# A fused attention and two-MLP kernel: the second half of w1 decoded earlier and kept in DRAM, the second half of w2 decoded beside the last two units

## The chip, the core and the metric

The kernel runs on one core of one Trainium2 chip. TensorE (PE) multiplies, VectorE (DVE), ScalarE (ACT) and GpSimd (POOL) work on tiles, and SyncE (SP) issues nearly all DMAs, in order, from one queue. The metric is the time of one execution on the device in microseconds (us).

## The reference, cut to what matters

```python
attn_out = attention(q, k, v, M_prev, z_prev, beta)      # 4 x 8 heads x 576 x 64
x = attn_out.transpose(0, 2, 1, 3).reshape(2304, 512)
h = x @ w_in                                             # 512 x 2048
g = h * tanh(softplus(h))
x = g @ w_out                                            # 2048 x 512
a, b = x @ w1, x @ w2                                    # 512 x 1024 each
out = ((a * b) @ w3) @ w_out2                            # 1024 x 1024, 1024 x 512
```

Inputs and weights of the two MLPs come as float64 words, and the kernel works on float32. "Decoding" a piece of a weight means turning its 128x512 words of 64 bits into float32.

## The kernel before, in words

All matrix products are made from split numbers: a weight or an activation is kept as a high part and a low part, and each product is three matmuls (high by high, low by high, high by low).

*Decoding.* `decode` loads one piece (`draw`, 512 KB) from SP's queue, runs six DVE instructions on it (lines 113, 115, 117, 120, 124, 126) and one add on POOL (line 131). What follows depends on the use. `to_split` makes the high part (line 76) and the low part (line 79) on POOL, straight into a weight tile. `to_dram` makes both on POOL, into the raw buffer itself, and writes them to a DRAM scratch tensor (line 161), from where `from_dram` loads them later (line 657) with no further work.

*First stage.* Attention over 16 pairs of heads; it leaves x, split, in two tiles with the tags `xs0` and `xs1`.

*Second stage.* Units (g, n): g is one of four quarters of w_in and w_out, n one of six chunks of 384 tokens. `emit_h` makes h for a unit (48 matmuls), ACT and DVE turn it into y, `emit_x2` multiplies by w_out for the unit before it (48 matmuls) and DVE adds the result into `x2` (line 604). Beside the units of a quarter the next quarter's eight pieces are decoded (`nextq`), and at fixed units one or two pieces of `predecode` (`pre`): w_out2, the first half of w1 and the first half of w2, 16 pieces in all, into DRAM. So a unit has two or three decodes.

*Last quarter (g = 3).* There are no more quarters to decode. Instead `fold` multiplies w3 by w_out2 in 17 steps: a step decodes a piece of w3 (`da`), transposes it on PE (line 628), splits it (`w3h`, `w3l`), and multiplies the piece of the step before by `o2` (w_out2, loaded from DRAM, line 614). The finished rows go through `wo` to `w_dram`, and are loaded again as `wft` (line 702). `steps(beside, 1)` in `emit_h` and `emit_x2` advances the fold. When the unit n = 3 comes, the slot `xs0` is free, and the first halves of w1 and w2 are loaded into it (`w_slot(0)`).

*Last stage.* For each of 40 pairs (chunk c of 512 tokens, m one of 8 blocks of 128 columns), `emit_ab` makes a and b (24 matmuls into one of two `psA` tiles), ACT and DVE multiply and split them into one of six slots of `ring`, and `emit_out`, five pairs later, multiplies by `wft`. The pairs m = 4 to 7 need the second halves of w1 and w2 (tile `w12t`, slot `xs1`). In the kernel before these eight pieces are decoded by `rest`, two at the last `emit_x2` and two after each of the pairs k = 0, 1 and 2, first the four of w2, then the four of w1:

```python
        if k < 3:
            steps(rest, 1)
```

The split of the next token chunk (`x2s`, line 731) lies in memory that the decode buffers hold until `rest` is done.

*Order.* The framework moves instructions: each engine's order is set by a model of the run in which ready work of an earlier place in the program goes first, unless `tc.issue_after` holds it back. A change in one stage can therefore move instructions in the others. On the chip each engine then works through its list in order and waits on semaphores.

Of the kernel before, what the change touches and what calls it, by code (L numbers as in the profile page):

```python
# [9 lines left out]
F32 = mybir.dt.float32  # L10
# [11 lines left out]
def fused_kernel(ctx: ExitStack, tc, q, k, v, M_prev, z_prev, beta, w_in, w_out, w1, w2, w3, w_out2, out):  # L22
    nc = tc.nc
    B, H, S, D = q.shape
    NT, DM = out.shape
# [4 lines left out]
    KD = DM // 128  # L30
# [5 lines left out]
    NCH = NT // CH  # L36
# [4 lines left out]
    dram = ctx.enter_context(tc.tile_pool(name="dram", bufs=1, space=bass.MemoryType.DRAM))  # L41
# [14 lines left out]
    def f(ap):  # L56
        return ap.bitcast(F32)
# [26 lines left out]
    def steps(gen, n):  # L84

        for _ in range(n):
            next(gen, None)
# [5 lines left out]
    WN = 512  # L93
# [40 lines left out]
    def run(jobs, n):  # L134

        jobs = list(islice(jobs, n))
        for (a, r), (_, done) in zip(decode([src for src, _ in jobs]), jobs):
            done(a, r)

    def by_two(jobs):  # L140
        for _ in range(4):
            run(jobs, 2)
            yield

    def words(w, r0, c0):
        return w[r0:r0 + 128, c0:c0 + dec["w"]].bitcast(I32)

    def to_split(hi, lo):
        def done(a, r):
            pool_round(hi, a)  # L150
            sub(lo, a, hi, nc.gpsimd)

        return done

    def to_dram(dst):
        def done(a, r):
            w = dec["w"]
            hi, lo = r[:, 0:w], r[:, w:2 * w]
            pool_round(hi.bitcast(F32R), a)
            nc.gpsimd.tensor_tensor(out=lo.bitcast(F32R), in0=a, in1=hi, op=ALU.subtract)  # L160
            dm(out=dst.rearrange("i p c -> p i c"), in_=r.rearrange("p (i c) -> p i c", i=2))

        return done
# [11 lines left out]
    w1_dram = dram.tile([2, DM, WN], F32, name="w1_dram")  # L175
    o2_dram = dram.tile([2, FF2, DM], F32, name="o2_dram")
    w2_dram = dram.tile([2, DM, WN], F32, name="w2_dram")

    def predecode():
        for w, wd in ((w_out2, o2_dram), (w1, w1_dram), (w2, w2_dram)):  # L180
            for c in range(w.shape[0] // 128):
                yield words(w, 128 * c, 0), to_dram(wd[:, 128 * c:128 * c + 128, 0:WN])

    def second_half(t):
        for i, w in ((1, w2), (0, w1)):
            for c in range(KD):
                yield words(w, 128 * c, WN), to_split(t[:, i, 0, c], t[:, i, 1, c])

    xl = {}

# [464 lines left out]
    def from_dram(t, d):  # L655
        for i in range(2):
            dm(out=f(t[:, i]), in_=d[i].rearrange("(k p) f -> p k f", p=128))

    def w_slot(s):
        t = xp.tile([128, 2, 2, KD, 512], F32R, tag=f"xs{s}", name="w12t", padded_shape=[128, 2, 2, KD, S])  # L660
        if s == 0:
            for i, wd in enumerate((w1_dram, w2_dram)):
                from_dram(t[:, i], wd)
        w1t[s], w2t[s] = t[:, 0], t[:, 1]
        return t

    folding = fold()
    pre0 = nextq = iter(())
    prev = None
    w1t, w2t = [None, None], [None, None]  # L670
    for u in [(g, n) for g in range(NQ) for n in range(NCH)]:
        g, n = u
        last = g == NQ - 1
        if u not in gt:
            if last and fpool[0] is None:
                dk.close()
                fpool[0] = fk.enter_context(tc.tile_pool(name="fp", bufs=1))
                decoder(fk, 2, 2)
            y = early.pop(u) if u in early else emit_h(u, folding if last and n > 0 else iter(()))
        if last and n == 3:  # L680
            w_slot(0)
        if prev is not None:
            with tc.issue_after(emit_x2(prev, folding if last and n > 0 else pre0)):
                split = split_y(u, y)
        with tc.issue_after(split):
            if n == 0 and not last:
                run(pre, 2)
            elif not last:
                run(nextq if n < 4 else chain(islice(nextq, 1), islice(pre, 1)), 2)
            if g in (1, 2) and n in (0, 2):  # L690
                run(pre, 1)
        if last and n == 0:
            steps(folding, 1)
        if not last and n == 0:
            nextq = load_quarter(g + 1)
        prev = u
# [4 lines left out]
    for s in range(4):  # L701
# [1 line left out]
            out=f(wft[:, 1, 2 * s:2 * s + 2]),  # L703
            in_=w_dram[256 * s:256 * s + 256, :].rearrange("(k p) f -> p k f", p=128),
        )
    rest = by_two(second_half(w_slot(1)))
    emit_x2(prev, islice(rest, 1))
    wk.close()


# [61 lines left out]
    for k, (c, m) in enumerate(work):  # L772
        if k == 4:
            fk.close()
            late = ctx.enter_context(tc.tile_pool(name="late", bufs=1))
            x2s = late.tile([128, 2, KD, 512], F32R, name="x2s")
            xs_[1] = x2s[:, 0], x2s[:, 1]
        emit_ab(k)
        if k in (3, 4):
            for i in range(4 * k - 12, 4 * k - 8):  # L780
                nc.scalar.copy(out=wft[:, 0, i], in_=f(wft[:, 1, i]))
                sub(wft[:, 1, i], f(wft[:, 1, i]), wft[:, 0, i])
        if k < 3:
            steps(rest, 1)
        if m == 5 and c + 1 < len(spans):
            split_x2(c + 1)
        if k >= LAG:
            emit_out(k - LAG)
# [34 lines left out]
```

## Time and profile before

| what | value |
|---|---|
| runs of the kernel | 1024.27, 1026.0 and 1026.07 us, median 1026.0 us |
| the profiled execution | 1024.95 us, its span 1023.2 us |
| PE busy | 977.8 us (96%) |
| DVE busy | 612.0 us (60%) |
| ACT busy | 500.7 us (49%) |
| POOL busy | 339.0 us (33%) |
| granted TensorE clock, mean | 0.988 |

The span is what the profiler sees from the first to the last instruction; the execution's own time is 1.75 us longer. Busy shares are means over stages with different limits, so the sections below go by stretches of the span. Times in the rows are microseconds from the span's start unless marked ns.

### The profile page before, as it was taken

The page shows a single profiled execution, that of the slowest core. Times are in us where ns is not written, and L with a number is a line of the kernel's source. Part 1 is how long each engine was busy: PE and PEld are TensorE (multiplying, and loading weights), DVE is VectorE, ACT ScalarE, POOL GpSimd, SP SyncE. Part 2 cuts the span into 40 slices and gives each one's busy share as a digit, 9 for nine tenths or more (in the row PEclk, how much of TensorE's full clock was granted, in tenths as well). Part 3 has the DMA queues.
Part 4 walks back from the last instruction along what each step waited for, and adds up shares of the span by engine and source line. Part 5 has one row for each costly group of instructions (what it writes and reads, how often), then busy time and mean ns, then how long its engine had stood idle before and what let it go on. Part 6 is the DMA issues. An engine that isn't in the chain of part 4 may idle for free.

```text
span 1023.2 us, 15086 instructions
## 1 busy us (share of the span) xinstructions
PE 977.8 (96%) x5584; PEld 829.1 (81%) x5584; DVE 612.0 (60%) x1364; ACT 500.7 (49%) x1016; POOL 339.0 (33%) x345
## 2 busy tenths in 40 slices
PE   5888999999899999999999999999979999999998
PEld 2555555566799999999999999988758888888897
DVE  4887667667685759885987567667973121121111
ACT  5577888885655555556565544442313221221212
POOL 6675555433555254544454112112540000000000
PEclk9899999999999999999999999999999999999999
DMA  7343333311232124223331662222410000100101
GB/s 157 96 110 71 71 87 74 77 27 42 103 124 80 65 83 145 98 89 106 121 103 63 247 232 80 75 78 101 156 41 1 21 21 1 42 1 1 42 1 62
DMA packets 93626, 81.73 MB, mean 80 GB/s; under 512 B 68720, under 2 KB 72816, under 8 KB 93552
## 3 DMA queue, kind: packets, MB, share of 16 engines
q1 hardware_dynamic: 92224, 80.44, 25.3%
q8 instruction: 44, 0.72, 0.3%
q10 hardware_dynamic: 1328, 0.33, 0.2%
q14 instruction: 30, 0.25, 0.1%
HBM read 65.54 MB, written 15.20 MB: 79 GB/s over the span
## 4 chain that ended last, share of the span: by engine, by line
PE 71%; DVE 12%; ACT 11%; DMA 2%; POOL 2%; issue 2%; SPq 0%; POOLq 0%; ACTq 0%; DVEq 0%
PE psA L63 37%; PE psX L63 16%; PE psF L63 14%; ACT s L378 5%; ACT pt L430 3%; DVE s L368 2%; PE psF L66 2%; DMA draw<-in_moe_w_dram 1%; DVE da L120 1%; PE psX L66 1%; DVE xt L79 1%; POOL da L131 1%; DVE draw L126 1%; DVE da L117 1%; DVE s L373 1%
## 5 line engine op out<-in xcount | busy, mean ns | idle before, releaser
L63 PE MATMUL psA<-xt,wqt 128*128 128x384 f32 x1152 | 207.5, 335 | 0.2
L131 POOL TENSOR_TENSOR da<-da,draw 128x512 f32<-128x512 f32 x72 | 102.2, 1426 | 312.8 <-DVE draw L126 261.9
L63 PEld LDWEIGHTS psA<-xt,wqt 128*128 128x128 f32 x1152 | 200.0, 188 | 2.4 <-DVE y L487 0.8
L63 PE MATMUL psX<-gh,wqt 128*128 128x384 f32 x480 | 122.4, 335 | 1.1 <-DVE x L604 1.1
L749 DVE TENSOR_TENSOR bs<-bs,psA 128x512 f32<-128x512 f32 (+1 forms) x40 | 25.3, 633 | 160.0 <-ACT bs L748 160.0
L63 PE MATMUL psA<-x2h,w12t 128*128 128x512 f32 (+1 forms) x384 | 107.1, 356 | 6.9 <-DVE bs L749 4.6
L748 ACT COPY bs<-psA 128x512 f32<-128x512 f32 (+1 forms) x40 | 21.8, 545 | 162.1 <-PE psA L63 152.2
L378 ACT ACTIVATE s<-s,acc 128x512 f32<-128x512 f32 (+2 forms) x144 | 85.5, 603 | 12.8 <-DVE acc L373 12.7
L63 PE MATMUL psA<-x2s,w12t 128*128 128x512 f32 x384 | 89.6, 389 | 0.0
L63 PEld LDWEIGHTS psX<-gh,wqt 128*128 128x128 f32 x480 | 86.9, 188 | 2.3 <-DVE x L604 1.4
L477 ACT ACTIVATE y<-psA 128x384 f32<-128x384 f32 x96 | 42.0, 490 | 91.1 <-PE psA L63 91.0
L63 PEld LDWEIGHTS psA<-x2h,w12t 128*128 128x128 f32 x384 | 68.3, 189 | 20.7 <-DVE bs L749 5.0
L63 PEld LDWEIGHTS psA<-x2s,w12t 128*128 128x128 f32 x384 | 72.1, 188 | 14.9
L373 DVE CUSTOM_DVE_ANT_0 s<-psA,mask 128x512 f32<-128x512 f32 (+2 forms) x144 | 63.4, 483 | 34.4 <-PE psA L63 34.3
L63 PE MATMUL psX<-gl,wqt 128*128 128x384 f32 x240 | 80.3, 335 | 0.0
L66 PEld LDWEIGHTS psF<-ident,s 128*128 128x128 f32 x400 | 46.3, 147 | 40.8 <-ACT pt L430 24.8
L63 PE MATMUL psF<-gh,wqt 128*128 128x384 f32 x288 | 73.1, 334 | 0.0
L66 PE MATMUL psF<-ident,s 128*128 128x128 f32 x400 | 63.2, 292 | 9.9 <-ACT pt L430 7.5
L487 DVE TENSOR_TENSOR y<-y,psA 128x384 f32<-128x384 f32 x96 | 48.7, 549 | 34.9 <-ACT y L485 34.9
L63 PE MATMUL psA<-room,w12t 128*128 128x512 f32 (+1 forms) x192 | 68.0, 354 | 0.0
L368 POOL TENSOR_SCALAR s<-s,sum,ogp 128x128 f32<-128x128 f32 (+1 forms) x64 | 53.1, 840 | 37.2 <-DVE sum L364 37.2
L430 ACT COPY pt<-psF 128x512 f32<-128x512 f32 (+1 forms) x112 | 56.8, 546 | 16.0 <-PE psF L66 16.0
(114 smaller groups left out, 1878.3 us busy)
## 6 DMA issues: line engine op xcount, KB each, us to landing
draw<-in_moe_w_dram SPq DMA_DIRECT2D x32, 512.0 KB, 3.8
draw<-in_moe_w_out_dram SPq DMA_DIRECT2D x24, 512.0 KB, 3.5
draw<-in_moe_w_in_dram SPq DMA_DIRECT2D x16, 512.0 KB, 4.0
out_dram<-ob SPq DMA_DIRECT2D x18, 256.0 KB, 2.0
raw<-in_q_dram SPq DMA_DIRECT2D x32, 128.0 KB, 2.8
raw<-in_v_dram SPq DMA_DIRECT2D x32, 128.0 KB, 2.6
o_dram<-draw SPq DMA_DIRECT2D x8, 512.0 KB, 2.8
w_dram<-draw SPq DMA_DIRECT2D x8, 512.0 KB, 2.8
```

Of the source, the lines that this page charges most:

```text
L63: tail[0] = nc.tensor.matmul(o, lhsT=l, rhs=r, start=start, stop=stop).ins
L66: tail[0] = nc.tensor.transpose(o, src, ident).ins
L79: return (eng or nc.vector).tensor_tensor(out=dst, in0=src, in1=f(hi), op=ALU.subtract)
L131: nc.gpsimd.tensor_tensor(out=a, in0=a, in1=lw.bitcast(F32), op=ALU.add)
L368: (nc.gpsimd if x in ON_POOL else nc.vector).tensor_scalar(out=s, in0=s, scalar1=d["sum"][:, x:x + 1], scalar2=og[:, x:x + 1], op0=ALU.mul ...
L373: nc.vector.tensor_tensor_reduce(out=s, in0=o, in1=m, op0=ALU.add, op1=ALU.min, scale=-scale, scalar=init, accum_out=a,)
L378: nc.scalar.activation(out=s, in_=s, func=AF.Exp, scale=-1.0, bias=a, accum_out=r)
L430: nc.scalar.copy(out=t[:, 0:n], in_=o[:, 0:n])
L477: nc.scalar.activation(out=y[m // 2][:, m % 2], in_=hp[m], func=AF.Tanh, scale=0.5)
L487: nc.vector.tensor_tensor(out=y[i][:, j], in0=y[i][:, j], in1=hp[2 * i + j], op=ALU.mult)
L748: nc.scalar.copy(out=bs, in_=pb)
L749: nc.vector.tensor_tensor(out=bs, in0=bs, in1=pa, op=ALU.mult)
```

## The change

The second half of w1 joins `predecode`: four more pieces are decoded in the second stage and written to a new DRAM tensor `w1b_dram`, and for them the units with a third decode are moved and become eight instead of four. `w_slot(1)` is now called at the last unit, n = 5, and loads w1's second half from DRAM. Only the four pieces of w2's second half are still decoded into their tile: two beside the second half of the `emit_x2` of the unit (3, 4), between two fold steps (the new generator `both`), and two in the `emit_x2` of (3, 5). The last stage no longer decodes.

```diff
     def by_two(jobs):
-        for _ in range(4):
+        for _ in range(2):
             run(jobs, 2)
             yield
...
+    w1b_dram = dram.tile([2, DM, WN], F32, name="w1b_dram")
...
     def predecode():
         for w, wd in ((w_out2, o2_dram), (w1, w1_dram), (w2, w2_dram)):
             for c in range(w.shape[0] // 128):
                 yield words(w, 128 * c, 0), to_dram(wd[:, 128 * c:128 * c + 128, 0:WN])
+        for c in range(KD):
+            yield words(w1, 128 * c, WN), to_dram(w1b_dram[:, 128 * c:128 * c + 128, 0:WN])
 
     def second_half(t):
-        for i, w in ((1, w2), (0, w1)):
-            for c in range(KD):
-                yield words(w, 128 * c, WN), to_split(t[:, i, 0, c], t[:, i, 1, c])
+        for c in range(KD):
+            yield words(w2, 128 * c, WN), to_split(t[:, 1, 0, c], t[:, 1, 1, c])
...
             for i, wd in enumerate((w1_dram, w2_dram)):
                 from_dram(t[:, i], wd)
+        else:
+            from_dram(t[:, 0], w1b_dram)
...
+    def both(a, b):
+        while True:
+            next(a, None)
+            yield
+            next(b, None)
+            next(a, None)
+            yield
...
         if last and n == 3:
             w_slot(0)
+        if last and n == NCH - 1:
+            rest = by_two(second_half(w_slot(1)))
+            beside = both(folding, rest)
         if prev is not None:
-            with tc.issue_after(emit_x2(prev, folding if last and n > 0 else pre0)):
+            with tc.issue_after(emit_x2(prev, beside if last and n > 0 else pre0)):
                 split = split_y(u, y)
...
-            if g in (1, 2) and n in (0, 2):
+            if g in (1, 2) and n == 0 or not last and n in (2, 4):
                 run(pre, 1)
...
-    rest = by_two(second_half(w_slot(1)))
-    emit_x2(prev, islice(rest, 1))
+    emit_x2(prev, rest)
     wk.close()
...
-        if k < 3:
-            steps(rest, 1)
```

The orders show three places. The first is PE's list in the last stage, where the first products with `wft` (`emit_out`) stand. Before, it is after the fourth pair of `emit_ab`, and the next pair's matmuls wait for POOL, which makes `w12t`:

```order
L63 MATMUL psA<-x2h,w12t 128x512
L63 MATMUL psX<-wft,room 128x512 [waits Activation_49]
L63 MATMUL psX<-wft,room 128x512 [waits DMAHW4_49,DVE_49]
L63 MATMUL psX<-wft,room 128x512
L63 MATMUL psF<-wft,room 128x512 [waits PE_49]
L63 MATMUL psF<-wft,room 128x512
L63 MATMUL psA<-x2h,w12t 128x512 [waits DVE_49,Pool_49]
L63 MATMUL psA<-room,w12t 128x512
L63 MATMUL psA<-x2h,w12t 128x512 [waits Pool_49] x2
```

In the changed kernel the same rows stand after the sixth pair (144 matmuls of `emit_ab` ahead of them instead of 96):

```order
L63 MATMUL psA<-x2h,w12t 128x512
L63 MATMUL psX<-wft,room 128x512 [waits Activation_49]
L63 MATMUL psX<-wft,room 128x512 [waits DMAHW5_49,DVE_49]
L63 MATMUL psX<-wft,room 128x512
L63 MATMUL psF<-wft,room 128x512 [waits PE_49]
L63 MATMUL psF<-wft,room 128x512 x2
L63 MATMUL psX<-wft,room 128x512 x3
L63 MATMUL psF<-wft,room 128x512 [waits PE_49,Activation_49]
L63 MATMUL psF<-wft,room 128x512 x2
L63 MATMUL psA<-x2h,w12t 128x512 [waits DVE_49]
```

Between the first `emit_ab` matmul and these rows PE now has three groups of 12 fold matmuls and two sets of four transposes; before it had two groups and one set, so the fold ends one step later.

The second place is DVE's list near the third pair of the last stage. Before, two decodes run there, with the split of `wft` between them, and three more follow:

```order
L113 TENSOR_SCALAR da<-draw 128x512
L126 SCALAR_TENSOR_TENSOR draw<-draw 128x512
L115 TENSOR_SCALAR da<-da 128x512
L117 TENSOR_SCALAR da<-da 128x512
L120 SCALAR_TENSOR_TENSOR da<-draw,da 128x512
L79 TENSOR_TENSOR wft<-wft 128x512 x2
L124 TENSOR_SCALAR draw<-da 128x512
L749 TENSOR_TENSOR bs<-bs,psA 128x512
```

Now these are the last two decodes, both of w2, and `wft` comes behind them:

```order
L113 TENSOR_SCALAR da<-draw 128x512
L764 TENSOR_TENSOR bs<-bs,psA 128x512
L126 SCALAR_TENSOR_TENSOR draw<-draw 128x512
L115 TENSOR_SCALAR da<-da 128x512
L79 TENSOR_TENSOR room<-bs,room 128x512
L117 TENSOR_SCALAR da<-da 128x512
L79 TENSOR_TENSOR w3l<-psF,w3h 128x512
L120 SCALAR_TENSOR_TENSOR da<-draw,da 128x512
L124 TENSOR_SCALAR draw<-da 128x512
L126 SCALAR_TENSOR_TENSOR draw<-draw 128x512
L764 TENSOR_TENSOR bs<-bs,psA 128x512
```

The third place is SP's list at the start of the last quarter. Before, the first piece of w3 (`draw`) is loaded ahead of `o2`:

```order
L161 DMA w_dram<-draw 128x2x512 [waits DMAHW6_49,DVE_49,Pool_49]
L109 DMA draw<-in_moe_w_dram 128x1024 [waits DMAHW7_49,DMAHW5_49,DMAHW0_49]
L614 DMA o_6195<-o_dram 128x4x512 [waits PE_49]
L614 DMA o_6195<-o_dram 128x4x512 x3
L109 DMA draw<-in_moe_w_dram 128x1024
```

Now the last write of `w1b_dram` stands there, and the first piece of w3 follows the four loads of `o2`:

```order
L161 DMA w1b_dram<-draw 128x2x512 [waits DMAHW6_49,DVE_49,Pool_49]
L616 DMA o_6248<-o_dram 128x4x512 [waits PE_49]
L616 DMA o_6248<-o_dram 128x4x512 x2
L616 DMA o_6248<-o_dram 128x4x512 [waits DMAHW4_49]
L109 DMA draw<-in_moe_w_dram 128x1024 [waits DMAHW7_49,DMAHW0_49]
L109 DMA draw<-in_moe_w_dram 128x1024
```

## Rows read from the trace of the kernel before

**Rows 1.** Busy us (count) of PE, PEld, DVE, ACT, POOL; clock, DMA share, GB/s

```profile
708.20:773.20 65.00, 57.79 (x246) 44.51 (x245) 51.29 (x74) 16.02 (x30) 28.93 (x24) 1.00 0.26 89
773.20:838.20 65.00, 65.00 (x288) 53.87 (x287) 15.95 (x24) 16.98 (x29) 0.00 (x0) 1.00 0.05 17
```

**Rows 2.** Who PE waited for, 708 to 775 us: total, times, longest

```profile
PE psA L63 <- DVE bs L749: 4.6, 3, 3.0
PE psA L63 <- POOL w12t L76: 2.1, 3, 1.5
PE psX L63 <- DVE wft L79: 0.4, 1, 0.4
```

**Rows 3.** PE's timeline: start, length, what, [idle before]

```profile
569.48 8.48 PE L63 MATMUL psA<-xt,wqt 128*128 128x384 f32 x48
...
708.19 0.61 PE L63 MATMUL psA<-x2h,w12t 128*128 128x512 f32 x2
...
714.77 0.60 PE L628 MATMUL psF<-ident,da 128*128 128x128 f32 x4
715.12 0.70 PE L63 MATMUL psF<-o,w3h 128*128 128x512 f32 x2
...
724.77 0.39 PE L63 MATMUL psF<-o,w3l 128*128 128x512 f32 x1
...
736.62 0.73 PE L63 MATMUL psX<-wft,room 128*128 128x512 f32 x2 [0.35 <-DVE wft L79]
...
767.61 0.50 PE L63 MATMUL psA<-x2h,w12t 128*128 128x512 f32 x1 [3.05 <-DVE bs L749]
```

**Rows 4.** POOL's timeline: the fifth and the eighth piece for `w12t`

```profile
742.17 1.61 POOL L79 TENSOR_TENSOR w12t<-da,w12t 128x512 fp32r<-128x512 f32 x1
...
762.49 1.29 POOL L79 TENSOR_TENSOR w12t<-da,w12t 128x512 fp32r<-128x512 f32 x1
```

**Rows 5.** ACT's timeline: the split of the next token chunk

```profile
763.81 2.18 ACT L731 CAST x2s<-x 128x512 fp32r<-128x512 f32 x4 [16.91 <-POOL w12t L79]
```

**Rows 6.** DVE's timeline: splits of `wft`, and the end of the fifth decode

```profile
734.79 2.38 DVE L79 TENSOR_TENSOR wft<-wft 128x512 fp32r<-128x512 f32 x2
...
738.62 0.68 DVE L126 SCALAR_TENSOR_TENSOR draw<-draw 128x512 f32<-128x512 uint32 x1
```

**Rows 7.** The same view: two units of the second stage, by half units

```profile
421.70:430.00 8.30, 8.30 (x50) 8.30 (x49) 8.13 (x12) 4.73 (x8) 4.54 (x4) 1.00 0.13 50
430.00:438.30 8.30, 8.20 (x47) 7.88 (x46) 8.20 (x14) 4.78 (x6) 5.78 (x6) 1.00 0.53 177
438.30:446.60 8.30, 8.30 (x50) 8.30 (x49) 6.83 (x15) 4.30 (x6) 2.07 (x2) 1.00 0.07 29
446.60:454.90 8.30, 8.30 (x50) 8.30 (x49) 5.49 (x10) 5.85 (x9) 4.56 (x5) 1.00 0.36 128
```

**Rows 8.** Waits of PE's weight loads, second stage (272 to 590 us): the whole answer

```profile
PEld psA L63 <- DVE y L487: 0.8, 2, 0.4
```

**Rows 9.** DVE's timeline: one decode, and POOL's at the same time

```profile
428.94 0.42 DVE L113 TENSOR_SCALAR da<-draw 128x512 int32<-128x512 int32 x1
429.40 1.42 DVE L115 TENSOR_SCALAR da<-da 128x512 f32<-128x512 f32 x1
...
429.11 1.43 POOL L131 TENSOR_TENSOR da<-da,draw 128x512 f32<-128x512 f32 x1 [1.10 <-DVE draw L126]
```

**Rows 10.** SP's timeline at the start of the last quarter

```profile
569.33 0.35 SPq L109 DMA_DIRECT2D draw<-in_moe_w_dram  x1
569.73 3.46 SPq L614 DMA_DIRECT2D o<-o_dram  x4
573.23 21.48 SPq L109 DMA_DIRECT2D draw<-in_moe_w_dram  x3
```

**Rows 11.** Busy time by stretch again: the end of the `o2` loads

```profile
584.00:588.00 4.00, 4.00 (x25) 4.00 (x24) 3.93 (x10) 0.32 (x2) 0.00 (x0) 1.00 0.59 231
```

**Rows 12.** PE's only noted wait from 590 to 708 us

```profile
PE psX L63 <- DVE x L604: 1.1, 1, 1.1
```

More of the change, by code (lines that the diff above doesn't have):

```diff
@@ L673, in fused_kernel @@
         last = g == NQ - 1
+        beside = folding
         if u not in gt:
```

## The prediction

> **What bounds the kernel now.** I read the busy time by stretch first. In the next 65 us of the last stage PE runs 288 matmuls without a gap, 65 / 288 = 0.226 us each; in the 65 us with which the stage begins it runs 246 [rows 1]. So PE is the bound nearly everywhere, and the one place where it is not lies at the start of the last stage, where DVE is busy 51.3 of 65 us and POOL still works. The deficit is 42 matmuls or 9.5 us. Four of the 246 are transposes, which together take 0.35 us (from 714.77 to the next matmul at 715.12 [rows 3]) and not 0.9, so about 0.5 us more is lost: **10.0 us**. The list of PE's waits accounts for 7 us of it, in seven single waits: for DVE's `bs` (4.6), for POOL's `w12t` (2.1), for `wft` (0.4) [rows 2]; the rest are slower starts after such waits. The reader should see that POOL is the smaller name but the root. The last piece of `w12t` is done at 762.49 + 1.29 = 763.8 us [rows 4], and in that moment ACT starts `x2s`, which it had stood at for 16.9 us because its memory is that of the decode buffers [rows 5]; behind it in ACT's queue stand the `bs` copies, and the 3.05 us wait at 767.61 is for the `bs` product [rows 3]. Before that, DVE splits `wft` in the middle of the fifth of the eight decodes, which ends at 739.3 us [rows 6]. Elsewhere PE waits once for 1.1 us, in the last unit but one [rows 12], and in the second stage only its weight loads wait, twice for 0.4 us [rows 8].
>
> **The change, part by part.**
>
> *Removed from the last stage: the whole stall, if nothing takes its place, −10.0.* No decode of w1 remains there, and `x2s` is freed as soon as the last of two w2 pairs is done. I checked the three things that could now be late, on a clock that starts with the first `emit_ab` matmul, T (before: 708.19 [rows 3]). On PE's new list stand ahead of the first `wft` product 144 + 36 matmuls and 8 transposes: 180 × 0.226 + 0.7 = T + 41.4; the last fold matmul is 49 matmuls earlier, at T + 30.3, and the fifth pair (k = 4), first to use the second halves, begins there too. Its last w2 piece is needed nine matmuls in, T + 32.5 to 33.
>
> First, that piece. On DVE its decode stands where the fifth of eight stood (the last w3 piece has slipped in ahead, in the third's place), and the fifth was finished at 742.17 + 1.61 = 743.8, T + 35.6 [rows 4], which would be 2.5 us late. But DVE gave 2.4 us of that time to splits of `wft` [rows 6], which now stand behind the decode, against one split `w3l` of about 0.7 (as line 126, of the same shape [rows 6]). And POOL's add in the third place no longer waits for the low part of the piece before, 1.6 us (the length of that at 742.17), so the raw buffer comes free that much earlier. 743.8 − 2.4 + 0.7 − 1.6 = 740.5, T + 32.3: just in time. Bounds 0 and 2.5 us.
>
> Second, `wft`. Before, from the last fold matmul (724.77 + 0.39) to the matmul that got `wft` (736.62) it took 11.5 us [rows 3]. Now there are 41.4 − 30.3 = 11.1. So this chain, which had ample time before, is just met: 0.4 us late if it runs as before, earlier if ACT and DVE are freer. Bounds 0 and 2.
>
> Third, the first `bs`. Its DVE place behind two decodes is unchanged, while one fold group fewer stands between the pairs; I take 0 to 0.5 us.
>
> Of these three together I take **+0.8**, 0.4 for `wft` and 0.4 for the other two, near their low ends, because a wait for one gives the others time; together at most 2.5.
>
> *Added to the second stage: four decodes with their writes.* PE's work there is unchanged, so the cost is what DVE delays. Eight units now have three decodes, each followed by one with two; before there were four such units. In two units (33.2 us) with five decodes DVE is busy 8.13 + 8.20 + 6.83 + 5.49 = 28.65 us [rows 7]: the unit with three is full, the next gives the backlog back, 4.5 us remain, and a pattern that alternates 3 and 2 does not build up a lag. What such a pair costs shows in the second row: 47 matmuls instead of 50, 3 × 0.17 = 0.5 us [rows 7], with a wait of 0.4 at the weight load [rows 8]; two of the four pairs have that wait, the others none that is listed. So a pair costs 0 to 0.5 us, I take 0.3: **+1.2**, bounds 0 and 2.0. POOL is busy 16.95 of the 33.2 us, 3.4 per decode, and the DMA share is 0.07 to 0.53 [rows 7], so POOL's added work and the four writes of 512 KB lie in idle time.
>
> A rule is to be weighed here. While POOL adds (429.11 to 430.54), DVE's line 115 takes 1.42 us beside 0.42 for the similar instruction ahead of it [rows 9]: it ends 0.3 us after POOL, so it stood still. The Trainium skill says so too (SBUF — State Buffer, section "Who interferes with whom"): DVE and GpSimd share one pair of ports under an exclusive lock, and the later one is blocked for the other's whole instruction. By that rule at its fullest, with all of POOL's 3.4 us blocking, an added decode would cost DVE as much again, and the sum would be the third rival's. The full units of rows 7 already contain such collisions, and I use what they show.
>
> *Moved: the start of the fold.* SP loaded the first w3 piece at 569.33, ahead of the four loads of `o2`, 1 MB each [rows 10]. Now it is behind it, and behind the write of the last w1 piece, which the added decode can make later. The queue with `o2` and the next pieces drains in the stretch 584 to 588 at a share of 0.59, so about 586.4 [rows 11]. The first piece then lands at 586 to 590; with 4.0 us for the decode (16.33 us of a unit with three less 12.32 of one with two [rows 7]) and 1.4 for POOL's add [rows 9] it is ready at 592 to 596. PE's new list has its transposes 143 matmuls behind the start of the `emit_h` at 569.48, whose 48 matmuls take 8.48 us with the last one's tail of about 0.3 [rows 3], or 0.174 each: 569.5 + 143 × 0.174 = 594.4. 596 would be 1.6 us late, and DVE's `w3l` behind the next decode can add to that: bounds 0 and 2.5 us. I take **+0.8**, a third of it, since the early end needs only that the write does not hold SP.
>
> *Moved: `w_slot(1)`.* Its two loads of 1 MB wait for the last `emit_h`, which on PE's list ends 96 + 46 matmuls before T (96 × 0.174 + 46 × 0.226 = 27 us), and move in about 8 us (5 MB in 16.7 us at the `o2` loads, 569.7 to 586.4 [rows 10, 11]). They are needed at T + 33. What stands behind them on SP is a `wo` write and the next w3 piece; the fold has one step's slack. Cost 0, and if the cover were gone, those 8 us late at one w3 piece would cost PE at most the wait of one fold step, 3 to 5 us; that is in the second rival. The wait of 1.1 us in the last unit [rows 12] may shrink or stay: 0.
>
> *Sum*, against the profiled execution's own time: 1024.95 − 10.0 + 0.8 + 1.2 + 0.8 = **1017.8 us**. That execution lies 1.05 us below the median of the three runs (1026.0) and within their spread of 1.8 us; I leave the forecast on its scale.
>
> **The rivals.**
>
> 1. *The gap closes* (the forecast): 1017.8, own range 1014 to 1020.5.
>
> 2. *A new wait takes a good part of the gain.* The fold is now one step later against `emit_ab`, and it is followed by a chain through PE, ACT, SP, DRAM, ACT and DVE that has 11.1 us where it took 11.5. If SP's queue holds the last `wo` or the `wft` loads behind two pieces (512 KB each, 1.7 us at the pace of the `o2` loads), or the fold's start loses its 2.5 us and the w2 piece its 2.5, 3 to 6 us come back: 1021 to 1023.5. For it: no slack in the chain. Against it: DVE has 5 us less to do between T + 20 and T + 40.
>
> 3. *DVE becomes the bound of the second stage* (the other side). It decides at the point where five decodes no longer fit into two units: 28.65 us would have to become more than 33.2, that is 0.9 us more per decode. Then each added decode costs its DVE time, at most the 4.0 us above: 1024.95 − 10.0 + 16 = 1031. The collisions with POOL are what could bring it about; the rows of such units [rows 7] speak against it, since the last half unit of each pair has 2.8 us idle; for it, that the raw buffers (three) are held longer by writes.
>
> 4. *The stall only moves.* The loss at 762 to 768 was `x2s` behind the decode buffers; if `wft` or `x2s` holds `bs` in the same way, 8 to 10 us stay: 1024 to 1027. Against it: `x2s` needs its first use only at the ninth pair, about T + 58, and can start at about T + 42.
>
> **How the numbers follow.** Chances: forecast 0.68, rival 2 0.19, rival 3 0.05, rival 4 0.08. A measurement of this kernel can tell about 0.2% (2 us) from no change. Rivals 1 and 2 end below 1024: faster 0.87. Rival 4 is mostly within 2 us of 1026: same 0.08. Rival 3: slower 0.05. The range leaves out rivals 3 and 4, a corner of rival 2, and the far end of the gain: low end 1024.95 − 10.0 − 1.1 (the wait of rows 12 gone too) = 1013.9 with all additions nil; high end the sum of the bounds, 1024.95 − 10.0 + 2 + 2.5 + 2.5 = 1022: **1014 to 1022**.
>
> **What would show it.** In the changed profile the 65 us behind the first `emit_ab` matmul should hold 275 matmuls or more, mostly `emit_ab`, with no wait for `w12t` and none over 1 us for `bs`; `x2s` should start about 42 us behind it, not 55. POOL's last instruction should end 31 us behind it. In the second stage PE's weight loads should wait some 1 to 2 us in total, over four or more places. The first fold transposes, near 594, show a wait under 2.5 us. Wrong would be: a wait of several us for `wft` at the first `emit_out`, a run of DVE at full share over two whole units, or a wait of PE for POOL's `da` at the start of the fold that later steps repeat.

## The result, and the profile after

The changed kernel takes **1017.13 us** (median of four runs, 1016.81 to 1017.69) against 1026.03 us of the kernel before (four runs, 1024.27 to 1026.17). The ratio of the means is 0.9918, 95% interval 0.9901 to 0.9935, or 8.4 us less; between the medians it is 8.9 us. The profiled execution took 1017.02 us, with a span of 1015.2 us and a mean granted clock of 0.986. The forecast was 1017.8 us.

The busy time by stretch, of the first and the second 65 us of the last stage, in the columns of [rows 1]:

```profile
707.00:772.00 65.00, 65.00 (x292) 53.78 (x291) 39.29 (x65) 21.28 (x39) 14.97 (x13) 1.00 0.20 65
772.00:837.00 65.00, 65.00 (x289) 53.81 (x288) 13.65 (x20) 14.31 (x24) 0.00 (x0) 1.00 0.05 17
```

Where PE had run 246 matmuls in 57.79 busy us, it now runs 292 without a gap, and the list of PE's waits from 700 us to the end of the span is empty, for the matmuls and for the weight loads. Four engines' timelines show how close the three things came that the prediction looked at: PE's first matmul of the stage (T), the last piece of `w12t` on POOL, the first load of `wft` on SP, `x2s` on ACT, and PE's first product with `wft`.

```profile
707.03 0.62 PE L63 MATMUL psA<-x2h,w12t 128*128 128x512 f32 x2
...
738.11 1.29 POOL L79 TENSOR_TENSOR w12t<-da,w12t 128x512 fp32r<-128x512 f32 x1
...
737.89 0.38 SPq L718 DMA_DIRECT2D wft<-w_dram  x1
...
746.48 2.18 ACT L746 CAST x2s<-x 128x512 fp32r<-128x512 f32 x4
...
748.81 0.84 PE L63 MATMUL psX<-wft,room 128*128 128x512 f32 x3
```

The last piece is written at 739.4 us, T + 32.4 (predicted: T + 32.3), and PE comes to the tenth matmul of the fifth pair, the first that needs it, at T + 32.9; the `wft` product starts at T + 41.8 (41.4); `x2s` starts at T + 39.5 (42).

In the second stage the change costs more than it was given. The waits there (272 to 590 us) of PE and of its weight loads, which answer to [rows 8]:

```profile
PE psA L63 <- DVE y L489: 1.4, 2, 0.9
...
PEld psA L63 <- DVE y L489: 4.0, 7, 1.2
```

The longer of PE's two, on its timeline:

```profile
402.82 1.50 PE L63 MATMUL psA<-xt,wqt 128*128 128x384 f32 x7 [0.86 <-DVE y L489]
```

A finer measure is the distance between the starts of successive `emit_h` blocks (48 matmuls) on PE's timeline. An undisturbed unit takes 16.64 us; what a unit takes beyond that is lost. The decodes of a unit run beside the `emit_h` blocks that stand one and two units further on, so the column of a unit with three decodes holds what is lost over the second and third block behind its own, in us (the last column holds one block only):

| unit with three decodes | (0,2) | (0,4) | (1,0) | (1,2) | (1,4) | (2,0) | (2,2) | (2,4) |
|---|---|---|---|---|---|---|---|---|
| before | | | 0.07 | 0.40 | | 0.08 | 0.36 | |
| after | 0.07 | 0.36 | 1.16 | 0.34 | 0.37 | 0.79 | 0.37 | 0.26 |

The sums are 0.91 and 3.72: **2.8 us** for the four decodes. The four added pairs, (0,2), (0,4), (1,4) and (2,4), lose 1.06 us of it. The two pairs at n = 0, which had a third decode before as well, go from 0.15 to 1.95, and the two at n = 2 from 0.76 to 0.71. So the larger part of the cost, 1.8 us, lies where no decode was added.

Last, the start of the fold: SP's timeline, and the fold's first transposes on PE's.

```profile
563.74 10.64 SPq L161 DMA_DIRECT2D w1b_dram<-draw  x2
574.43 3.10 SPq L616 DMA_DIRECT2D o<-o_dram  x4
...
597.38 0.66 PE L630 MATMUL psF<-ident,da 128*128 128x128 f32 x4 [0.75 <-POOL da L131]
```

The loads of `o2`, which began at 569.73 [rows 10], begin at 574.43, because the last write of w1 stands ahead of them. The transposes wait 0.75 us. The wait of 1.1 us in the last unit but one [rows 12] is gone.

The balance of the two profiled spans, 1023.2 and 1015.2: up to the first `emit_h` of the table −0.8 (285.69 and 284.88, in attention, which the change doesn't touch); the second stage +2.8; from the last `emit_h` of that count (569.48 [rows 3] and 571.48) to T −3.2; from T to the end 315.0 and 308.2, −6.8. Some 3.1 us of fold matmuls have moved from ahead of T to behind it, so the last two are like for like −0.1 and −9.9.

### The profile page after: what moved, and what is told of

Same layout as the page of the kernel before. It is cut to its first block, busy times and chain, and to the rows that moved or that the text cites. A ratio compares the mean times of both kernels' runs of the same rounds, so it can differ in the third digit from the quotient of the medians.

```text
span 1015.2 us, 15110 instructions
## 1 busy us (share of the span) xinstructions
PE 976.4 (96%) x5584; PEld 829.6 (82%) x5584; DVE 624.7 (62%) x1364; ACT 499.9 (49%) x1016; POOL 339.2 (33%) x345
## 4 chain that ended last, share of the span: by engine, by line
PE 58%; DVE 18%; ACT 12%; DMA 4%; POOL 3%; issue 3%; SPq 2%; POOLq 0%; ACTq 0%; DVEq 0%
PE psA L63 32%; PE psX L63 12%; PE psF L63 11%; ACT s L380 5%; ACT pt L432 3%; DVE da L120 2%; DVE da L117 2%; DVE draw L124 2%; DVE s L370 2%; DVE da L115 2%; DVE y L489 1%; PE psF L66 1%; DVE draw L126 1%; DMA draw<-in_moe_w_dram 1%; DVE gl L79 1%
## 5 line engine op out<-in xcount | busy, mean ns | idle before, releaser
L375 DVE CUSTOM_DVE_ANT_0 s<-psA,mask 128x512 f32<-128x512 f32 (+2 forms) x144 | 63.4, 482 | 33.0 <-PE psA L63 32.9
L497 ACT CAST gh<-y 128x768 fp32r<-128x768 f32 x48 | 40.0, 837 | 52.9 <-DVE y L489 28.9
L370 POOL TENSOR_SCALAR s<-s,sum,ogp 128x128 f32<-128x128 f32 (+1 forms) x64 | 53.3, 843 | 36.6 <-DVE sum L366 36.6
```

What stands on the lines that cost most here:

```text
L370: (nc.gpsimd if x in ON_POOL else nc.vector).tensor_scalar(out=s, in0=s, scalar1=d["sum"][:, x:x + 1], scalar2=og[:, x:x + 1], op0=ALU.mul ...
L375: nc.vector.tensor_tensor_reduce(out=s, in0=o, in1=m, op0=ALU.add, op1=ALU.min, scale=-scale, scalar=init, accum_out=a,)
L497: nc.scalar.copy(out=gh, in_=y[i])
```

## The experiments

The theory: the gap closes because only four pieces are left to decode in the last stage, so the last is written before PE asks for it; and the price is what DVE delays in the second stage. The rivals for the gain were the earlier place of w2's decode, and `x2s`, whose memory the decode buffers held; for the price, the other things that the four decodes bring (writes, loads, SP's order). Times are compared with the kernel before on the same chip: 1025.02 us for the run with six pieces and its control, 1024.77 us for all the others.

### What closed the gap

**w2 late again**, w1 as changed:

```diff
-            beside = both(folding, rest)
...
-    emit_x2(prev, rest)
+    emit_x2(prev, islice(rest, 1))
...
+        if k < 1:
+            steps(rest, 1)
```

> The changed kernel, but w2's second half decoded as late as before (one pair at the last emit_x2, one pair after k = 0). Theory (the gap of the last stage came from eight decodes in a row and from x2s behind them; four of them fit beside the first four emit_ab pairs): 1017 us, 1016 to 1018.5, no wait of PE for w12t above 1 us. Rival (it is the early place of w2's decode, between the fold steps, that closes the gap): a wait for w12t or bs at k = 4 returns and the time is 1019 to 1022.

Measured: 1016.41 us, ratio 0.9921 (0.9906 to 0.9936), and no wait of PE in the last stage. The last piece is written at 744.07 us, T + 37.0; PE comes to it later than in the changed kernel (the tenth matmul of the fifth pair at T + 36.3, the twelfth, first to use the low part, at T + 37.7), because the order now has fold matmuls inside that pair. So the early place of w2's decode, half of the change's text, brings nothing that can be measured.

**w1 late, w2 early as changed**:

```diff
-            yield words(w1, 128 * c, WN), to_dram(w1b_dram[:, 128 * c:128 * c + 128, 0:WN])
...
-        for c in range(KD):
-            yield words(w2, 128 * c, WN), to_split(t[:, 1, 0, c], t[:, 1, 1, c])
+        for i, w in ((1, w2), (0, w1)):
+            for c in range(KD):
+                yield words(w, 128 * c, WN), to_split(t[:, i, 0, c], t[:, i, 1, c])
...
+        if k < 2:
+            steps(rest, 1)
```

> The other half alone: w2's second half decoded early as in the changed kernel, w1's second half decoded in the last stage after it (pairs at k = 0 and 1), nothing added to the second stage. Theory: the second stage's cost of 2.8 us falls away, but about 5 to 7 us of the 10 us gap stay, because the last piece of w1 is ready some 45 us behind the first emit_ab matmul and is needed at 33: 1017.1 - 2.8 + 6 = 1020, 1018 to 1023. Rival (the place of w2 closes the gap and w1 hardly counts): 1014 to 1015.5.

Measured: 1025.14 us, ratio 1.0004 (0.9994 to 1.0013). This missed: the whole gap stays. POOL's and ACT's timelines of this run:

```profile
756.36 1.68 POOL L131 TENSOR_TENSOR da<-da,draw 128x512 f32<-128x512 f32 x1 [5.39 <-DVE draw L126]
...
762.63 1.29 POOL L79 TENSOR_TENSOR w12t<-da,w12t 128x512 fp32r<-128x512 f32 x1
...
763.96 2.18 ACT L743 CAST x2s<-x 128x512 fp32r<-128x512 f32 x4 [13.66 <-POOL w12t L79]
```

The first of the eight pieces is written 10 us earlier than in the kernel before (705.4 and 715.6), the last at 763.9 as against 763.8 [rows 4]. Between the pieces DVE waits for a decode buffer (2.35 us at 734.16), then splits `wft` for 5.53 us from 744.29, and POOL waits for DVE, as the first row shows. A start that comes 10 us earlier was used up on the way.

**No wait for the pieces**: the kernel before, whose last four column blocks read the first half's tiles.

```diff
-        for o, w in ((pb, w2t[m // 4]), (pa, w1t[m // 4])):
+        for o, w in ((pb, w2t[0]), (pa, w1t[0])):
```

> The kernel before with the products of the last four column blocks of w1 and w2 read from the first half's tiles (the wrong columns): all eight pieces are still decoded in the last stage, but no matmul waits for them. Theory A: the 10 us gap is the matmuls' wait for the decoded pieces; then 1015.5 to 1018 us, with no wait for w12t left. Theory B, from the run in which w1's four pieces alone kept the whole gap: what counts is the time at which the last piece is written, since the second copy of x2 takes the decoder's memory and stands on ScalarE behind it (763.8 in the kernel before); then a wait for x2s or for what stands behind it on ScalarE and VectorE takes the place of the wait for w12t, the sum of waits in the last stage falls by 0 to 4 us, and the run takes 1021 to 1026.

Measured: 1017.17 us, ratio 0.9926 (0.9912 to 0.9940), on the side of theory A. The last stage takes 308.3 us in place of 315.0. PE's waits from 690 us to the end:

```profile
PE psA L63 <- DVE bs L749: 2.4, 2, 2.0
PE psX L63 <- DVE wft L79: 0.2, 1, 0.2
```

The largest of them on PE's timeline, and `x2s` on ACT's:

```profile
745.77 0.50 PE L63 MATMUL psA<-x2h,w12t 128*128 128x512 f32 x1 [2.01 <-DVE bs L749]
...
764.92 2.18 ACT L731 CAST x2s<-x 128x512 fp32r<-128x512 f32 x4 [4.28 <-POOL w12t L79]
```

`x2s` starts as late as ever (T + 57.0, before T + 55.6) and nothing waits for it: the wait of 3.05 us for `bs` at 767.61 [rows 3] is gone. So 6.7 of the 9.9 us come back when no matmul needs the late pieces. The list of PE's waits had named `w12t` for 2.3 us only, 2.1 for the high parts [rows 2] and one wait more:

```profile
PE psA L63 <- POOL w12t L79: 0.2, 1, 0.2
```

The other 3.2 us stay here, 2.4 of them as waits for `bs`, while DVE still has all eight decodes and the `wft` splits.

**Six pieces left**: two of w1's four in the last stage, and the two units with n = 0 given back.

```diff
-        for c in range(KD):
+        for c in range(2):
             yield words(w1, 128 * c, WN), to_dram(w1b_dram[:, 128 * c:128 * c + 128, 0:WN])
...
+        for c in range(2, KD):
+            yield words(w1, 128 * c, WN), to_split(t[:, 0, 0, c], t[:, 0, 1, c])
...
-            if g in (1, 2) and n == 0 or not last and n in (2, 4):
+            if not last and n in (2, 4):
```

> Only w1's first two row blocks are decoded in the second stage, as third decodes of the units with n = 2 and 4; the two with n = 0 are given back, and w1's last two row blocks are decoded in the last stage behind w2's four: six pieces there, against four of the change and eight of the kernel before. Second stage: 1.7 to 2.0 us less loss by the two units with n = 0 (1.16 and 0.79 in the changed kernel). Last stage, theory (what makes the gap is how many pieces are left, each some 6 us behind the one ahead): in the kernel before the sixth piece was written 45.8 us behind the first product and the eighth 55.6, and 10 us were lost; the sixth then costs 0 to 2 us, and the run takes 0 to 2 us less than the control beside it. Rival (any w1 piece that is left there stands behind the splits of wft on VectorE and behind wft on SP, as in the run with w2 early and w1 late, which kept the whole gap): the last stage loses 4 to 9 us, and the run takes 2 to 7 us more than the control.

Measured: 1016.52 us, ratio 0.9915 (0.9901 to 0.9930). The control beside it, the changed kernel again,

> The changed kernel as the control of the run beside it: a ratio of 0.990 to 0.993 to the kernel before.

took 1016.89 us, 0.9921 (0.9908 to 0.9933); the two can't be told apart. PE's waits from 590 us on:

```profile
PE psF L632 <- POOL da L131: 1.2, 1, 1.2
PE psA L63 <- POOL w12t L76: 1.0, 2, 0.6
```

The sixth piece is written at T + 40.8, and the list names 1.0 us of waits for it. Counted as the balance above counts, the loss is larger: the last stage takes 307.3 us with 24 fold matmuls in it, as before, where the changed kernel without its 3.1 us of moved matmuls takes 305.1. So with four pieces the last stage loses nothing, with six 2.2 us, with eight 9.9. That is a little beyond the theory's 0 to 2 us and far under the rival's 4 to 9. The second stage loses 1.2 us in place of the control's 3.5, the units (1,0) and (2,0) nothing at all, and the fold's start waits 1.2 us in place of 0.5. The three together would put the run 0.6 us behind its control, which is within the spread of both.

### What the four decodes cost

**Without them**: w1's second half is not decoded, and the first half is loaded again in its place.

```diff
-        for c in range(KD):
-            yield words(w1, 128 * c, WN), to_dram(w1b_dram[:, 128 * c:128 * c + 128, 0:WN])
...
-            from_dram(t[:, 0], w1b_dram)
+            from_dram(t[:, 0], w1_dram)
...
-            if g in (1, 2) and n == 0 or not last and n in (2, 4):
+            if g in (1, 2) and n in (0, 2):
```

> The changed kernel without the four added decodes of the second stage: the second half of w1 is not decoded at all, and the first half is loaded again in its place, so the kernel computes with wrong columns of w1. It measures what the four decodes cost. Theory (the unit pitch of the second stage shows 2.8 us, all of it by third decodes): 1017.1 - 2.8 = 1014.3, 1013.5 to 1015; starts of emit_h 16.64 us apart but for the four old units. Rival (the instruction order of the changed program costs it, not the decodes): 1016.5 to 1017.5.

Measured: 1015.10 us, ratio 0.9908 (0.9893 to 0.9922). The second stage loses 0.95 us, as before, and the wait of 1.1 us in the last unit but one is back. From the first `emit_h` of the table to the end it takes 728.1 us, the changed kernel 730.4 and its two controls 730.0 and 730.1. So of the 2.8 us some 2 reach the end of the run.

**The four decodes in the last quarter** in place of the second stage:

```diff
-            if g in (1, 2) and n == 0 or not last and n in (2, 4):
+            if g in (1, 2) and n in (0, 2):
...
+        if last and 0 < n < 5:
+            with tc.issue_after(split):
+                run(pre, 1)
```

> The changed kernel with the four pieces of w1's second half decoded beside the units n = 1 to 4 of the last quarter instead of in the second stage. Theory (DVE has some 8 us free in each of these units of 26 us, four in the second stage's): the second stage loses no more than before, 1014.5 us, 1013.5 to 1016. Rival (the two raw buffers there are shared with the fold, the write to DRAM holds one, and the fold falls behind): PE waits for da or w3l in the last quarter, or the fold ends later, and the time is 1016.5 to 1021.

Measured: 1023.86 us, ratio 0.9986 (0.9976 to 0.9996): above both ranges. The second stage is as before, but the decoder has only two raw buffers in the last quarter, and the loads of w3 stand behind the writes that hold these. From 590 to 700 us SP's loads wait 7.0 us for writes to `w1b_dram`, and DVE waits 14.0 us for loads, in the kernel before 4.4. The third row is PE's worst wait in the last quarter:

```profile
SPq L109 <- DMA w1b_dram<-draw: 7.0, 3, 2.4
...
DVE da L113 <- DMA draw<-in_moe_w_dram: 14.0, 4, 4.4
...
PE psF L630 <- DVE w3l L79: 3.6, 1, 3.6
```

and the stretch with it (columns of [rows 1]):

```profile
680.00:690.00 10.00, 6.37 (x20) 5.03 (x19) 8.92 (x17) 0.37 (x1) 1.30 (x1) 0.66 0.40 131
```

**Odd places**: the same eight units with three decodes, at odd n and none at n = 0.

```diff
-            if g in (1, 2) and n == 0 or not last and n in (2, 4):
+            if not last and n % 2 and u != (2, 5):
```

> The same twenty pieces, but the eight units with three decodes are those with odd n (without the last one ahead of the last quarter), and none has n = 0. Theory: what the second stage loses beyond 0.07 to 0.37 us a pair comes from the two units with n = 0, whose two writes hold SP just ahead of the next quarter's w_in draws; then the seventeen units lose 2.3 to 2.9 us in place of 3.7, the fold's first transposes wait under 0.3 us in place of 0.75, and the run takes 1015.0 to 1016.0 us. Rival: the loss belongs to the eight decodes wherever they stand (0.35 us each) or moves to the units with n = 5 and n = 1, and the run takes 1016.7 to 1018 us.

Measured: 1018.74 us, ratio 0.9944 (0.9932 to 0.9957); the control beside it,

> The changed kernel once more, as the control of the runs beside it: 1016.5 to 1018, a ratio of 0.991 to 0.993, with 3.7 us lost in the second stage's units over 16.64 us each and a fold start that waits 0.75 us.

took 1015.81 us, 0.9910 (0.9896 to 0.9923). Both theories missed. The units with n = 0 lose 0.1 us each, and the fold's first transposes don't wait, as expected. But the unit (0,1), the first with three decodes, loses 2.9 us:

```profile
318.90 1.31 PE L63 MATMUL psA<-xt,wqt 128*128 128x384 f32 x6 [2.66 <-DVE y L489]
```

DVE waits 1.7 us for POOL at one decode, at 299.42, and starts the third only at 312.06, so its `y` comes 2.7 us late. (This run reaches the table's first `emit_h` 1.1 us earlier than its control, which gives part of that back.) The other seven pairs lose 2.9 us together, and in the last quarter, where the fold's start no longer stalls, the wait of 1.1 us is back with one of 0.8 for `w3l` at the transposes of 617.37. From the last `emit_h` of the count to T it takes 137.1 us against 135.3 in the control.

**Four decodes more**: w1's second half decoded a second time into a tensor that nothing reads.

```diff
+        for c in range(KD):
+            yield words(w1, 128 * c, WN), to_dram(w1c_dram[:, 128 * c:128 * c + 128, 0:WN])
...
-            if g in (1, 2) and n == 0 or not last and n in (2, 4):
+            if g in (1, 2) and n in (0, 1, 3) or not last and n in (2, 4):
```

> The changed kernel with four more pieces in the second stage (w1's second half decoded a second time into a DRAM tensor that nothing reads), as third decodes of the units (1,1), (1,3), (2,1) and (2,3): in the quarters 1 and 2 six decodes then stand in some pairs of units, 39 us of VectorE work by the rates of the prediction against 33.2 us of matmuls. Theory: each such pair overfills VectorE (32.7 us and more with the other work), a lag builds over consecutive units of three, and four more pieces cost far more than the first four did (2.8 us): 8 to 20 us, 1025 to 1037. Rival: each piece costs what it cost before, 0.4 to 0.7 us, and the run takes 1018.5 to 1020.

Measured: 1037.17 us, ratio 1.0115 (1.0100 to 1.0131), 21.4 us above the control: the theory's side, just beyond the far end of its range. (The 39 us in the expectation was a slip: the prediction's rates give 28.65 + 4.0 = 32.65 us for six decodes, which would just fit.) A unit in the run of threes loses 2.4 to 3.9 us. The busy time by stretch of about two such units:

```profile
419.00:452.00 33.00, 28.92 (x150) 28.29 (x149) 32.59 (x51) 14.30 (x20) 16.57 (x15) 0.90 0.32 109
```

DVE's groups of instructions from 402 to 462 us (count | busy us, mean ns | idle), first of this kernel, then of the changed one:

```profile
L117 DVE TENSOR_SCALAR da<-da 128x512 int32<-128x512 int32 x9 | 8.1, 897 | 0.2
L115 DVE TENSOR_SCALAR da<-da 128x512 f32<-128x512 f32 x9 | 7.3, 812 | 0.1
L113 DVE TENSOR_SCALAR da<-draw 128x512 int32<-128x512 int32 x10 | 7.0, 700 | 0.1
```

```profile
L117 DVE TENSOR_SCALAR da<-da 128x512 int32<-128x512 int32 x9 | 5.9, 670 | 0.1
...
L115 DVE TENSOR_SCALAR da<-da 128x512 f32<-128x512 f32 x9 | 4.6, 527 | 0.0
...
L113 DVE TENSOR_SCALAR da<-draw 128x512 int32<-128x512 int32 x9 | 4.2, 480 | 0.0
```

DVE is full (32.59 of 33 us), and its instructions take longer on the mean. The mean durations of a decode's six instructions add up to 4.96 us here, 3.86 in the changed kernel, and 3.59 in the run without the four decodes (same window). The trace shows which of them take longer. Two lines of DVE with POOL idle, then the same two lines each behind the POOL instruction that was running when it started:

```profile
406.02 0.41 DVE L117 TENSOR_SCALAR da<-da 128x512 int32<-128x512 int32 x1
408.76 0.42 DVE L124 TENSOR_SCALAR draw<-da 128x512 int32<-128x512 int32 x1
...
411.06 1.42 POOL L131 TENSOR_TENSOR da<-da,draw 128x512 f32<-128x512 f32 x1 [6.17 <-DVE draw L126]
411.35 1.42 DVE L117 TENSOR_SCALAR da<-da 128x512 int32<-128x512 int32 x1
...
413.33 1.60 POOL L160 TENSOR_TENSOR draw<-da,draw 128x512 fp32r<-128x512 f32 x1
413.82 1.41 DVE L124 TENSOR_SCALAR draw<-da 128x512 int32<-128x512 int32 x1
```

The slow ones end 0.3 us behind POOL's instruction. Counted over the 60 us: 30 of a decode's instructions start with POOL idle and take 0.53 us on the mean, 25 start while a POOL instruction runs and take 1.18, and every one of these ends 0.28 to 0.55 us behind POOL's. In the changed kernel there are 42 (0.51 us) and 11 (1.17), in the run without the four decodes 47 (0.51) and 7 (1.19). So a decode's instructions have not become slower by themselves; more of them start beside POOL. An estimate from them: the 28.65 us for two units with five decodes [rows 7] leave 28.65 − 5 × 3.59 = 10.7 for everything else, and 10.7 + 6 × 4.96 = 40.5; two such units took 33.3 + 2.4 + 3.9 = 39.5 and 40.2 us.

## Why the prediction was right, and where a term was not

*The stall goes, −10.0.* Right: −9.9. That `w12t` was the root is shown for 6.7 us of it by the run that reads other tiles, and that the number of pieces left decides by the runs with four, six and eight. The link that the prediction drew for the largest wait, from the last piece by way of `x2s` to the 3.05 us for `bs`, is not borne out: in the run that reads other tiles `x2s` starts no earlier, and that wait is gone.

*The waits in the last stage, +0.8.* Measured 0. The estimate of the last w2 piece was right (T + 32.4), and PE got there at T + 32.9, as estimated: 0.5 us of room. DVE is done with the first two splits of `wft` at T + 36.6, 5.2 us ahead of PE's first product with it, so the slack there was larger than the prediction's chain showed. And PE never waits for `bs` once half of the decodes are gone.

*Four decodes in the second stage, +1.2, bounds 0 to 2.0.* This is the term that was mis-sized: 2.8 us in the profile, 2.7 and 2.6 in the controls (and 3.1 in the run with w2 late), beyond its upper bound; the weight loads wait 4.0 us in place of the 1 to 2 that the prediction gave as a sign. The step that failed is "a pattern that alternates 3 and 2 does not build up a lag". The four added pairs themselves cost 1.06 us, about what they were given. What they do to the pairs that were there already was put at nothing, and that is 1.8 us, all of it at n = 0.

That a lag is carried shows in the other columns of the table. The first pair of a series loses 0.05 to 0.09 us, in every run but that with the odd places; the second loses 0.35 to 0.41, and the later ones at other n than 0 mostly as much, although the unit between had two decodes. So a unit with two does not give all of the backlog back; units without a third decode between the pairs do. Before, two pairs and then two units of rest followed each other. In the change all eight pairs are one series, and the six-piece run, where the rest units at n = 0 are back, loses 0.05 to 0.08 and 0.26 to 0.40 in turn, as before.

What happens at n = 0 can be read from SP and DVE. Their timelines after the change:

```profile
382.55 1.62 SPq L161 DMA_DIRECT2D o_dram<-draw  x2
385.36 2.33 SPq L109 DMA_DIRECT2D draw<-in_moe_w_in_dram  x2
...
390.07 0.43 DVE L113 TENSOR_SCALAR da<-draw 128x512 int32<-128x512 int32 x1 [0.69 <-DMA draw<-in_moe_w_in_dram]
```

and SP's of the kernel before at the same place:

```profile
381.35 1.63 SPq L161 DMA_DIRECT2D o_dram<-draw  x2
384.16 1.71 SPq L109 DMA_DIRECT2D draw<-in_moe_w_in_dram  x2
```

The two writes go 1.2 us later, the next quarter's first loads stand behind them on SP, and DVE, which in the kernel before came no earlier than the load, now waits 0.69 us. Its `y` comes later, and PE waits 0.86 us at 402.82. But the late write alone does not do it. In the six-piece run SP has the same two writes at 382.55 and the next load at 385.36, and DVE waits longer still:

```profile
390.00 0.43 DVE L113 TENSOR_SCALAR da<-draw 128x512 int32<-128x512 int32 x1 [2.00 <-DMA draw<-in_moe_w_in_dram]
```

There the unit n = 0 has two decodes, and PE loses nothing. In the kernel before it has three, the load is not late, and the pair loses 0.07 us. In the run with odd places the third decode stands in the unit just ahead of n = 0, and the loss there is 0.1 us. So in these runs it takes both, a third decode and a load that comes late. At (2,0) of the changed kernel DVE's wait is shorter, and so is the loss:

```profile
491.43 0.43 DVE L113 TENSOR_SCALAR da<-draw 128x512 int32<-128x512 int32 x1 [0.34 <-DMA draw<-in_moe_w_in_dram]
```

In the four runs with the changed second stage (the change, its two controls, w2 late) the pair at n = 0 loses 0.41 to 0.50 us more than DVE waits for that load, with waits from 0.19 to 0.69: about what a later pair loses elsewhere, and the wait on top. The size of the wait itself was not varied on purpose.

The prediction weighed what the Trainium skill says of the ports that DVE and GpSimd share (SBUF — State Buffer, section "Who interferes with whom"), and went by the rows of full units. In the changed kernel the runs stand between the two: a decode has become 0.27 us longer than without the four pieces, not 3.4. In the run with four more they go the rule's way: the decodes grow by another 1.1 us each. The counts above say how: an instruction that starts beside POOL stands until POOL's has ended, in all three kernels, and what grows is the number of these, 7, 11 and 25 of some 54. POOL's time is not added in full because most instructions of a decode still start with POOL idle. So the third rival's mechanism is there. Five decodes in two units fitted, six did not, although busy time added up (32.65 of 33.2 us) would have let them.

*The start of the fold, +0.8.* Measured 0.75, and 0.45 and 0.51 in the controls. The write did hold SP: the loads of `o2` begin 4.7 us later, 2.7 us against PE's own work, which is 2.0 us later there (571.48 and 569.48).

*The wait of [rows 12], 0.* It went: −1.1, more than the fold's stall costs. In three runs where that stall is missing (without the four decodes, w1 late, odd places) the 1.1 us are back. But in the run with four decodes more, and in that with the decodes in the last quarter, neither shows, so that the one replaces the other is not shown.

*`w_slot(1)`, 0.* Two loads of 1 MB at the pace of the `o2` loads take 6.7 us, not the 8 of the prediction; no wait of PE for them is listed, so the term stays 0.

The sum held partly by luck, because errors offset each other: the second stage took 1.6 us more than its term, while the last stage's waits (0.8), the wait of [rows 12] (1.1) and 0.8 of attention came out lower. The controls' table begins at 283.75 and 285.41 us, so the last of these is the spread from one execution to another. In all −9.9 + 2.8 − 0.1 − 0.8 = −8.0 us of span, and 1.8 us lie around the span as before.

## What to carry to other kernels

A wait list names the last releaser, not the cause: here eight decoded pieces whose lateness cost PE at least 6.7 us showed as 2.3 us of `w12t` and twice that of `bs`. What is late was settled by letting nothing wait for it, and by varying how much of it is left.

Work that is spread over a nearly full engine should leave rest units: an average with 4.5 us of room in 33 carried a lag from unit to unit all the same, and SP's queue made a late write into a late load. Price also what the added work does to the full places that were there already: two thirds of the cost arose in them, and the same late load cost nothing where the unit had one decode less. Before moving work into "idle" time, ask also who else holds the buffers there; the last quarter had the idle time and not the buffers.

## What was not expected of the hardware

A decode's instruction that takes DVE 0.4 us with POOL idle took up to 1.5 us when it started beside a POOL instruction, and ended 0.3 us behind it. So the mean of line 113 was 700 ns with three decodes in unit after unit, beside 480 and 451 in the two kernels with fewer.

PE's granted clock fell with the gaps: 0.90 in the stretch of the row shown, where PE was idle 4.1 of 33 us, and 0.66 in the last quarter's stretch with 3.6 us of idle time in one piece. Both are means over a stretch, between the two levels of 1.2 and 2.4 GHz. In the changed kernel's last stage it stands at 1.00 throughout the two stretches.
